# 128 unused bytes per partition behind the weight tiles of a convolution and two MLP layers on one core

## The chip, the cores and the metric

The kernel runs on one core of one Trainium2 chip. The time is the device time of one execution in microseconds. Three timed runs of the kernel before gave 2313.24, 2318.7 and 2322.2 us; their median is 2318.7 us.

## The reference

The input x is 4 sequences of 4096 tokens with 192 channels. A causal convolution of 7 taps comes first, its taps a softmax over the kernel axis with one set for each of 8 heads of 24 channels; then two MLP layers with 2048 hidden units each. Cut to what is computed:

```
w = softmax(weight, axis=-1)                              # 8 heads x 7 taps
a[b, s, h] = sum_k w[h, k] * x_padded[b, s + k, h]        # 6 zeros ahead of each sequence
h = a @ moe_w_in                                          # 16384 x 192 @ 192 x 2048
y = (h - tanh(h)) @ moe_w_out                             # 2048 x 192
out = relu(y @ moe2_w_in) ** 2 @ moe2_w_out
```

The weights of the MLPs come as float64, x and the output are float32.

## The kernel before

The tokens are cut into 32 blocks of 512. A block goes through the convolution (mostly VectorE, taps with one multiply-add each, L230 and L233; for the first blocks TensorE with diagonal weights, L254), then layer 0, then layer 1. All products keep about float32 accuracy with operands in the type float32r: each operand is split into a high part and a rest, and three products stand for one: high by high, rest by high, high by rest. `gh` and `gl` are high part and rest of the activations (L417 on ScalarE, L419 on VectorE), `z` and `y` the split inputs of layer 0 and layer 1, `wIh`, `wIl` and `wO` the split weights.

The work is laid out in units. A unit is one layer, one block and one eighth of the hidden units (256 of them): 19 matmuls in each of two row halves of the TensorE array (`pe_step`). Each half reads 64 partitions, and the two halves' matmuls alternate in the instruction stream, so that they run beside each other as pairs (`matmul`, L359). The weight load belongs to each matmul. The order is written out by hand (`tc.manual_schedule`): between the matmuls of a unit stand its activation (`act`), its splits (`split`) and small lists of side work (`side`), such as loading and convolving later blocks, decoding float64 weights (`decode_ops`, L124 to L160, in the first 200 us only) and finishing an earlier block. Where one half hands a PSUM bank to the other, a no-operation on GpSimd carries the signal (`relay`); twice GpSimd zeroes the head of `xTa` and `xTb` for a new sequence (`halo`, L258).

DMAs all go by the SP queue: x into `xa`, `xb` and once into `t`, in pieces of 128 bytes (`load_a`, `load_b`); float64 weights into `st` (`load_w`); one half of `z` and `y` copied to the other 64 partitions, 4096 bytes each (`other_half`, L289); and the output from `ua` and `tu`, in pieces of 128 bytes (`store`, L442).

Tiles are given their place in SBUF in the order of the pools, each tile's size being rounded up to 32 bytes. In the program's list of allocations the tiles begin as follows (byte within each partition, and the remainder after division by 512; weights within a tile are read in blocks of 512 bytes from its start):

| tiles | first byte | remainder | size of one |
|---|---|---|---|
| wIh0, wIl0, wO0, wIh1, wIl1, wO1 | 16512, 28800, 41088, 65664, 77952, 90240 | 128 | 12288, wO 24576 |
| wt, taps, warm, mx, sm, th, den | 114816 to 115040 | | 4 to 56 |
| st (2), da (2) | 115072, 127360 | 384 | 6144, 3072 |
| xb, xa | 133504, 135552 | 384 | 2048 |
| xTb (2) | 137600, 139680 | 384, 416 | 2072 |
| xTa (2) | 141760, 143840 | 448, 480 | 2072 |
| accA, accB, z (2), y (3), t (3), gh (6), gl (6), ua, tu | 145920 to 223744 | 0 | 2048, z and y 8192 |

Of the kernel before, what the change touches and what calls it, by code (L numbers as in the profile page):

```python
# [10 lines left out]
F32 = mybir.dt.float32  # L11
# [19 lines left out]
def conv_mlp_mlp_kernel(ctx: ExitStack, tc: tile.TileContext, x, weight, w_in1, w_out1, w_in2, w_out2, out):  # L31
# [17 lines left out]
    P = 128  # L49
# [14 lines left out]
    wpool = ctx.enter_context(tc.tile_pool(name="wpool", bufs=1))  # L64
# [13 lines left out]
    for m in range(2):  # L78
        W.append(
            dict(  # L80
                Ih=wpool.tile([P, NP, CI], F32R, name=f"wIh{m}"),
                Il=wpool.tile([P, NP, CI], F32R, name=f"wIl{m}"),
                O=wpool.tile([P, NP, 2, 2 * D], F32R, name=f"wO{m}"),
            )
        )
    w_in = [w_in1, w_in2]
    w_out = [w_out1, w_out2]
    staged = {}
# [524 lines left out]
```

## Time and profile before

| | |
|---|---|
| median of three timed runs | 2318.7 us |
| lowest and highest of them | 2313.24 and 2322.2 us |
| span of the profiled execution | 2316.5 us |
| instructions | 50386 |
| TensorE matmul busy | 2301.4 us, 99% of the span |
| ScalarE busy | 1618.3 us, 70% |
| VectorE busy | 1468.0 us, 63% |
| GpSimd busy | 1.4 us |

The span is the time from the first to the last instruction of one profiled execution; the median of the timed runs is 2.2 us above it. Busy time of TensorE counts matmuls whose ends are modelled and overlap, so that 99% says that it hardly ever waited, not that it ran at its peak. PE is TensorE's matmul, PEld its weight load, DVE VectorE, ACT ScalarE, POOL GpSimd, SPq the queue that issues DMAs.

### The profile page before, as it was taken

The page shows a single profiled execution, that of the slowest core. Times are in us where ns is not written, and L with a number is a line of the kernel's source. Part 1 is how long each engine was busy: PE and PEld are TensorE (multiplying, and loading weights), DVE is VectorE, ACT ScalarE, POOL GpSimd, SP SyncE. Part 2 cuts the span into 40 slices and gives each one's busy share as a digit, 9 for nine tenths or more (in the row PEclk, how much of TensorE's full clock was granted, in tenths as well). Part 3 has the DMA queues.
Part 4 walks back from the last instruction along what each step waited for, and adds up shares of the span by engine and source line. Part 5 has one row for each costly group of instructions (what it writes and reads, how often), then busy time and mean ns, then how long its engine had stood idle before and what let it go on. Part 6 is the DMA issues. An engine that isn't in the chain of part 4 may idle for free.

```text
span 2316.5 us, 50386 instructions
## 1 busy us (share of the span) xinstructions
PE 2301.4 (99%) x19500; PEld 2046.9 (88%) x19500; DVE 1468.0 (63%) x2299; ACT 1618.3 (70%) x2866; POOL 1.4 (0%) x15
## 2 busy tenths in 40 slices
PE   9999999999999999999999999999999999999999
PEld 6777888888888888889999999999999999999998
DVE  8988666655576665666556665566665557665553
ACT  5577766677766777766777667776667776677766
POOL 0000000000000000000000000000000000000000
PEclk8999999999999999999999999999999999999999
DMA  5221111110110100101101011011111011110000
GB/s 128 64 75 36 22 22 17 22 23 14 22 22 17 26 15 17 27 13 26 22 11 26 17 22 22 15 22 22 17 22 24 13 22 18 21 22 15 13 13 15
DMA packets 216863, 57.78 MB, mean 25 GB/s; under 512 B 204336, under 2 KB 210480, under 8 KB 216624
## 3 DMA queue, kind: packets, MB, share of 16 engines
q1 hardware_dynamic: 216624, 54.56, 11.8%
q8 instruction: 154, 2.52, 0.5%
q14 instruction: 85, 0.70, 0.1%
HBM read 25.17 MB, written 12.58 MB: 16 GB/s over the span
## 4 chain that ended last, share of the span: by engine, by line
PE 96%; DVE 2%; ACT 1%; issue 0%; SPq 0%; DMA 0%; DVEq 0%; ACTq 0%
PE ph L359 45%; PE pA L359 31%; PE pB L359 20%; DVE da L138 0%; DVE da L134 0%; ACT gh L417 0%; DVE t L406 0%; DVE accA L233 0%; SPq L218 0%; ACT da L124 0%; DMA t<-in_x 0%; ACT t L408 0%; DVE da L129 0%; DVE gl L419 0%; DVE t L410 0%
## 5 line engine op out<-in xcount | busy, mean ns | idle before, releaser
L359 PE MATMUL pA<-gh,wO 64*128 64x512 f32 x4088 | 1281.7, 393 | 0.0
L419 DVE TENSOR_TENSOR gl<-t,gh 128x512 fp32r<-128x512 f32 x1024 | 682.3, 688 | 622.0 <-ACT gh L417 597.8
L359 PE MATMUL ph<-z,wIh 64*128 64x512 f32 x3072 | 990.0, 394 | 7.6 <-DVE t L406 6.4
L359 PE MATMUL ph<-y,wIh 64*128 64x512 f32 x3072 | 981.1, 392 | 0.6 <-DVE t L410 0.6
L359 PE MATMUL pB<-gh,wO 64*128 64x512 f32 x2044 | 802.3, 392 | 0.0
L359 PE MATMUL pA<-gl,wO 64*128 64x512 f32 x2044 | 801.4, 392 | 0.0
L359 PE MATMUL pB<-gl,wO 64*128 64x512 f32 x2044 | 800.4, 392 | 0.0
L359 PEld LDWEIGHTS pA<-gh,wO 64*128 64x128 f32 x4088 | 738.7, 185 | 47.4 <-issue 0.4
L417 ACT CAST gh<-t 128x512 fp32r<-128x512 f32 x1024 | 604.5, 614 | 97.8 <-DVE t L406 94.9
L359 PE MATMUL ph<-z,wIl 64*128 64x512 f32 x1536 | 604.3, 394 | 0.0
L359 PE MATMUL ph<-y,wIl 64*128 64x512 f32 x1536 | 601.6, 392 | 0.1
L359 PEld LDWEIGHTS ph<-z,wIh 64*128 64x128 f32 x3072 | 554.2, 186 | 48.7 <-ACT wIh L150 5.0
L359 PEld LDWEIGHTS ph<-y,wIh 64*128 64x128 f32 x3072 | 549.8, 185 | 36.3 <-DVE t L410 1.2
L405 ACT ACTIVATE t<-ph 128x512 f32<-128x512 f32 x512 | 305.4, 598 | 358.4 <-PE ph L359 278.9
L406 DVE TENSOR_TENSOR t<-ph,t 128x512 f32<-128x512 f32 x512 | 351.6, 689 | 199.2 <-ACT t L405 197.9
L359 PEld LDWEIGHTS pB<-gh,wO 64*128 64x128 f32 x2044 | 378.4, 185 | 36.2
L408 ACT ACTIVATE t<-ph 128x512 f32<-128x512 f32 x512 | 305.3, 596 | 147.3 <-PE ph L359 123.4
L359 PEld LDWEIGHTS pA<-gl,wO 64*128 64x128 f32 x2044 | 378.1, 185 | 26.7 <-DVE gl L419 0.4
L359 PEld LDWEIGHTS pB<-gl,wO 64*128 64x128 f32 x2044 | 378.4, 185 | 24.7
L412 ACT ACTIVATE t<-t 128x512 f32<-128x512 f32 x504 | 318.6, 632 | 16.0
L359 PEld LDWEIGHTS ph<-z,wIl 64*128 64x128 f32 x1536 | 285.6, 186 | 17.9 <-DVE wIl L155 0.7
L359 PEld LDWEIGHTS ph<-y,wIl 64*128 64x128 f32 x1536 | 284.1, 185 | 17.6 <-DVE wIl L155 0.4
(71 smaller groups left out, 707.0 us busy)
## 6 DMA issues: line engine op xcount, KB each, us to landing
z<-z SPq DMA_DIRECT2D x32, 256.0 KB, 2.9
y<-y SPq DMA_DIRECT2D x32, 256.0 KB
out<-ua SPq DMA_DIRECT2D x128, 64.0 KB, 1.9
xa<-in_x SPq DMA_DIRECT2D x124, 64.0 KB, 2.3
st<-in_moe_w_out SPq DMA_DIRECT2D x16, 384.0 KB, 6.3
xb<-in_x SPq DMA_DIRECT2D x64, 64.0 KB, 2.3
st<-in_moe_w_in SPq DMA_DIRECT2D x16, 256.0 KB, 3.2
out<-tu SPq DMA_DIRECT2D x64, 64.0 KB, 1.9
```

The source lines that it names most:

```text
L359: ins = nc.tensor.matmul(o, w, r, start=start, stop=stop).ins
L405: nc.scalar.activation(t, ph, AF.Tanh)
L406: nc.vector.tensor_tensor(t, ph, t, op=ALU.subtract)
L408: nc.scalar.activation(t, ph, AF.Relu)
L412: nc.scalar.activation(t, t, AF.Square)
L417: nc.scalar.copy(gh, t)
L419: nc.vector.tensor_tensor(gl, t, gh.bitcast(F32), op=ALU.subtract)
```

## The change

One tile is added to the pool of the weights, behind them and ahead of the small tiles of the taps. It has 32 float32 in each partition and is neither written nor read. No instruction is added.

```
                 O=wpool.tile([P, NP, 2, 2 * D], F32R, name=f"wO{m}"),
             )
         )
+    wpool.tile([P, 32], F32, name="pad")
     w_in = [w_in1, w_in2]
     w_out = [w_out1, w_out2]
     staged = {}
```

The weights stay where they are, and every tile behind them begins 128 bytes further on: the remainders 384, 416, 448, 480 and 0 of the table become 0, 32, 64, 96 and 128. PSUM is not touched.

## Rows read from the trace of the kernel before

**Rows 1.** The page: busy time of each engine, with share of the span and count.

```profile
PE 2301.4 (99%) x19500; PEld 2046.9 (88%) x19500; DVE 1468.0 (63%) x2299; ACT 1618.3 (70%) x2866; POOL 1.4 (0%) x15
```

**Rows 2.** The page: chain that ended last, share of the span by engine.

```profile
PE 96%; DVE 2%; ACT 1%; issue 0%; SPq 0%; DMA 0%; DVEq 0%; ACTq 0%
```

**Rows 3.** Stretches: length; busy us (instructions) per engine; granted TensorE clock; DMA.

```profile
30.00:40.00 10.00, 9.27 (x27) 6.49 (x26) 9.57 (x17) 4.54 (x8) 0.00 (x0) 0.50 0.50 142
...
100.00:200.00 100.00, 97.43 (x820) 75.91 (x818) 86.02 (x143) 76.84 (x141) 0.00 (x0) 1.00 0.26 70
200.00:400.00 200.00, 200.00 (x1726) 162.43 (x1724) 133.44 (x207) 139.37 (x248) 0.00 (x0) 1.00 0.12 22
400.00:1000.00 600.00, 600.00 (x5168) 487.33 (x5166) 369.06 (x572) 427.15 (x754) 0.20 (x2) 1.00 0.11 20
1000.00:1064.00 64.00, 64.00 (x554) 51.99 (x552) 36.74 (x56) 45.81 (x81) 0.00 (x0) 1.00 0.11 20
1064.00:2000.00 936.00, 936.00 (x8028) 897.61 (x8026) 584.77 (x906) 656.04 (x1157) 0.40 (x4) 1.00 0.11 20
2000.00:2280.00 280.00, 280.00 (x2403) 268.90 (x2401) 157.65 (x243) 198.12 (x347) 0.00 (x0) 1.00 0.07 15
```

**Rows 4.** Instructions in order around 800 us, TensorE: start us, duration us, engine, line.

```profile
800.12 0.39 PE L359 MATMUL pA<-gl,wO 64*128 64x512 f32 x1
800.12 0.39 PE L359 MATMUL ph<-z,wIl 64*128 64x512 f32 x1
800.35 0.40 PE L359 MATMUL pA<-gh,wO 64*128 64x512 f32 x1
800.35 0.40 PE L359 MATMUL ph<-z,wIh 64*128 64x512 f32 x1
800.59 0.39 PE L359 MATMUL pA<-gh,wO 64*128 64x512 f32 x1
```

**Rows 5.** The same around 1200 us.

```profile
1200.57 0.39 PE L359 MATMUL ph<-y,wIl 64*128 64x512 f32 x1
1200.61 0.40 PE L359 MATMUL pA<-gh,wO 64*128 64x512 f32 x1
1200.80 0.39 PE L359 MATMUL ph<-y,wIh 64*128 64x512 f32 x1
```

**Rows 6.** Instructions in order on GpSimd, in the middle of the span.

```profile
1064.28 0.10 POOL L258 MEMSET xTa<- 128x6 f32 x1 [564.94 <-PE pA L359]
```

**Rows 7.** Weight loads of the convolution on TensorE, in order; one moving read each.

```profile
9.14 0.19 PEld L254 LDWEIGHTS ph<-xTb,y 128*128 128x128 f32 x1 [0.24 <-ACT y L248]
...
13.00 0.19 PEld L254 LDWEIGHTS ph<-xTb,y 128*128 128x128 f32 x1 [0.24 <-issue]
...
14.58 0.19 PEld L254 LDWEIGHTS ph<-xTa,y 128*128 128x128 f32 x1 [0.24 <-issue]
...
19.31 0.19 PEld L254 LDWEIGHTS ph<-xTa,y 128*128 128x128 f32 x1 [0.24 <-issue]
```

**Rows 8.** Groups by line and shape: busy us, mean ns | idle before, releaser.

```profile
L419 DVE TENSOR_TENSOR gl<-t,gh 128x512 fp32r<-128x512 f32 x1024 | 682.3, 688 | 622.0 <-ACT gh L417 597.8 <-PE ph L359 0.5
L155 DVE TENSOR_TENSOR wIl<-da,wIh 128x384 fp32r<-128x384 f32 x16 | 8.9, 556 | 1.2 <-ACT wIh L150 1.2
L160 DVE TENSOR_TENSOR wO<-da,wO 128x256 fp32r<-128x256 f32 x16 | 6.7, 419 | 0.6 <-ACT wO L150 0.6
L160 DVE TENSOR_TENSOR wO<-da,wO 128x128 fp32r<-128x128 f32 x16 | 4.6, 285 | 0.0
```

**Rows 9.** DMA issues: count, KB each, median us from issue to landing.

```profile
z<-z SPq DMA_DIRECT2D x32, 256.0 KB, 2.9
st<-in_moe_w_in SPq DMA_DIRECT2D x16, 256.0 KB, 3.2
```

**Rows 10.** Who waited in the first 200 us: us in total, times, longest.

```profile
PE ph L359 <- DVE t L406: 6.4, 6, 3.2
DVE xTa L265 <- DMA t<-in_x: 3.2, 1, 3.2
```

More of the change, by code (lines that the diff above doesn't have):

```diff
@@ L85, in conv_mlp_mlp_kernel @@
         )
+    wpool.tile([P, 32], F32, name="pad")
     w_in = [w_in1, w_in2]
```

## The prediction

> **What bounds the kernel now.** I began with the busy times of the engines [rows 1] and the chain that ended last [rows 2]. TensorE is busy 99% of the span and holds 96% of the chain, VectorE 2%, ScalarE 1%, DMA nothing that shows. That names the engine; what one pair of matmuls costs it has to be read from a stretch without waits. The stretches [rows 3] give it: from 200 to 2280 us TensorE is busy in every microsecond, at a granted clock of 1.00 (the upper level, 2.4 GHz). In that time it starts 1726 + 5168 + 554 + 8028 + 2403 = 17879 matmuls, or 8940 pairs, one in each row half: 2080 us / 8940 = 232.7 ns a pair. So 90% of the time is one number times a count, and the change can matter in two ways: it alters that number, or it alters the first 200 us, in which TensorE does wait (6.4 us for VectorE's t in all, [rows 10]) and VectorE is busy 86.02 of 100 us [rows 3].
>
> The stretches show something else that I need for the range. The pair is not equally long everywhere: 600 / (5168 / 2) = 232.2 ns from 400 to 1000 us, 936 / (8028 / 2) = 233.2 ns from 1064 to 2000 us. The instructions in order show what differs. Around 800 us both matmuls of a pair start at the same hundredth [rows 4], around 1200 us one starts 0.04 us behind the other [rows 5]. The trace changes from the one to the other at about 1064 us, where GpSimd, which also carries the signals between the halves, zeroes the heads of two tiles [rows 6]. That nothing else sets it off I can't show from one execution.
>
> **The change part by part.** One tile is declared, and nothing reads or writes it. It removes, adds and moves no instruction, no DMA, no wait, so the sum over instructions is zero times anything. What is left is the place of the operands. Weights stay, at 128 bytes past a multiple of 512; everything behind them is read and written 128 bytes further on. Each kind of user of those tiles is a term:
>
> (a) TensorE's moving reads of z, y, gh and gl, from remainder 0 to remainder 128. No matmul of the trace in the long stretch reads a moving operand from remainder 128, so I bound it. Below: the 512 columns need 512 / 2.4 = 213.3 ns at the granted clock, which is 232.7 - 213.3 = 19.4 ns less, x 8940 = -173 us. Above: the slowest regular moving reads of the trace are those of the convolution, a weight load every 0.43 us [rows 7], 430 - 232.7 = 197 ns more, x 8940 = +1764 us. The ends are far apart, and the row that tells most about addresses is the upper one itself: those reads are of unsplit float32, which accounts for no address, but they start at xT plus 0, 4, ... 24 bytes, in tiles that begin at remainders 384 (xTb) and one of 448 and 480 (xTa). From 9.14 to 13.00 us there are 9 loads in 3.86 us, from 14.58 to 19.31 us 11 in 4.73 us: 0.429 and 0.430 us each, whatever the start. I take 0.
>
> (b) VectorE and ScalarE. VectorE's subtraction shows both kinds of address: between weight tiles and da (remainders 128 and 384) it takes 285, 419 and 556 ns for 128, 256 and 384 elements, some 136 ns for each 128 more, so 692 ns for 512; between t, gh and gl (remainder 0) the 512 take 688 ns [rows 8]. That is 0.6% at most, and of no certain sign: in the first 200 us, where VectorE is on the path, 0.006 x 200 = 1.2 us either way. Behind 200 us TensorE hides it: from 400 to 1000 us VectorE works 369 of 600 us and ScalarE 427 [rows 3], so ScalarE would have to become 600 / 427 = 1.4 times as slow before it bound anything. I take 0.
>
> (c) DMAs. z and y copies land 2.9 us after their issue and the largest loads of input weights 3.2 us [rows 9]; behind 200 us they are lost in the stretch without waits. In the first 200 us one DMA is waited for visibly, 3.2 us by VectorE's first use of t [rows 10]. So the bounds are -3.2 us (that wait gone) and +2.9 us (a copy twice as long, wholly on the path); the pieces of x keep their size and order, and I take 0.
>
> On (c) the Trainium skill has a rule, DMA: Bandwidth & Descriptors, "How a descriptor splits into AXI transactions": a transfer is cut at 256-byte boundaries, and one that starts off them needs a transaction more. By it the 4096-byte copies of z and y would go from 16 to 17 transactions, and the 2048-byte pieces of the weights, which now start off a boundary, from 9 to 8. No row here separates aligned from unaligned copies of one size. The sum by the rule, as an estimate from that page, would be 2.9 / 16 = 0.2 us more a copy and 3.2 / 9 = 0.4 us less a load, both under cover but for the first few, so some 2318 us instead of 2318.7 us.
>
> Sum: 2316.5 us of span plus 0. The timed median lies 2.2 us above that span, so the forecast is **2318.7 us**, as before.
>
> What one execution of the same program can do: if the halves stayed together to the end, the 8028 + 2403 matmuls behind 1064 us (5216 pairs) would each save 1.0 ns: 2316.5 - 5.2 = 2311.3 us. If they parted at 200 us, the 3724 pairs before 1064 us would each pay it: 2320.2 us. With the 2.2 us on top that is 2313.5 to 2322.4 us, and the timed runs reach from 2313.24 to 2322.2 us. That is the likeliest case's own range: a shift of addresses has no hold on it that I see, but the median of a few runs may land anywhere in it.
>
> **The rivals.**
>
> *Slower: load and moving read meet.* After the change the weights and the moving operands begin at the same remainder, 128, while a weight load (128 columns, 512 bytes) runs beside moving reads. If SBUF serves two readers at like offsets worse, every pair pays. The place is each pair of the long stretch, and the price is taken from the widest spacing of neighbouring pairs in the rows, 0.24 us (800.35 to 800.59, [rows 4]): 240 - 232.7 = 7.3 ns x 8940 = +65 us, 2384 us. It decides from 11.6 / 8940 = 1.3 ns a pair. For it: no row has the two at one remainder. Against it: each weight block starts at 128, 640, 1152 or 1664 in every 2048 bytes while moving tiles start at 512 there, and no row shows another spacing for one of the four; and the convolution's reads above don't care.
>
> *Faster: the present place is the bad one.* The pair stands 19.4 ns above its columns. If a part of that comes from where the operands lie, moving them may give it back, up to the -173 us of (a): 2145 us. Against it: the moving tiles lie in fourteen and more places of remainder 0, beside weights in four places of every 2048 bytes, and the trace keeps one spacing; nothing ties the 19.4 ns to an address. The Trainium skill speaks for it in a way: TensorE: Matmul & The Clock Gate, "Back-to-back issue gap", gives N/2.4 + 2.5 ns, so 215.8 ns here, and the rows show 232.7 ns. By that rule as the whole cost the time would be about 2318.7 - 8940 x 0.0169 = 2168 us, an estimate; the trace disagrees with it today, for a cause that it doesn't name.
>
> *The start shifts.* The first 200 us hold waits of several engines on each other, and TensorE's granted clock falls to 0.50 from 30 to 40 us [rows 3], in which 27 matmuls start where 86 start at full rate. A change of (b) or (c) by a microsecond could lengthen that idle time and cost one more such stretch: (86 - 27) / 2 x 0.2327 = +6.9 us, 2325.6 us, or save as much, 2311.8 us. Both are inside 0.5%.
>
> *The change does nothing of what it says:* an unused tile gets no room, or the rounding swallows it. Then the time is that of before, 2318.7 us, and no run of times tells it from the forecast; only the addresses would.
>
> **How the numbers follow.** A measurement of this kernel can tell about 0.5%, 11.6 us, from no change. The forecast has 0.79, with the idle tile inside it; the shifted start 0.05, on either side of it and within 0.5%; load and moving read 0.10; the present place 0.06. So faster 0.06, same 0.84, slower 0.10. The range must hold the likeliest case's 2313.5 to 2322.4 us and the shifted start on both sides, 2311.8 to 2325.6 us; together 0.84, so it need not reach the two outer rivals. I round it to 2311 to 2327 us, the upper side a little wider because the slower rival can also be small.
>
> **What would show it.** Right: 19500 matmuls as before, 232 to 233.5 ns a pair between 200 and 2280 us, VectorE's 512-element subtraction at 688 ns within a few, copies of z at about 2.9 us. The time at which one half falls behind the other may be another; then the time is off by 1.0 ns for each pair in between. Wrong: a pair spacing that is off by more than 1.3 ns in both kinds of stretch alike (an address matters to TensorE), or one operation of VectorE or ScalarE with another duration at the same shape while TensorE begins to wait behind 200 us.

## The result, and the profile after

The changed kernel takes 2261.22 us (2261.17 to 2261.57, four runs) beside 2315.97 us for the kernel before (2313.01 to 2322.2, four runs): a ratio of 0.9762, with a 95% interval from 0.9742 to 0.9782. It is faster by 2.4%, where no change was forecast. The profiled execution has a span of 2259.4 us, 57.1 us less.

The page of the changed kernel, busy time per engine and the chain that ended last; the number of instructions is the same as in [rows 1]:

```profile
PE 2242.7 (99%) x19500; PEld 1917.7 (85%) x19500; DVE 1464.7 (65%) x2299; ACT 1616.1 (72%) x2866; POOL 1.4 (0%) x15
...
PE 93%; DVE 4%; ACT 2%; issue 1%; SPq 0%; DMA 0%; DVEq 0%; ACTq 0%
```

TensorE is still the bound, and VectorE and ScalarE do the same work in nearly the same time. Busy time alone can't show what changed: its share is 99% in both. The stretches do. Each line has the stretch, its length, then busy time and number of instructions per engine (TensorE's matmul, its weight load, VectorE, ScalarE, GpSimd), granted clock and DMA:

```profile
0.00:200.00 200.00, 188.73 (x1412) 149.93 (x1414) 174.37 (x300) 130.47 (x248) 0.82 (x9) 0.96 0.32 83
...
200.00:400.00 200.00, 200.00 (x1768) 165.31 (x1766) 135.80 (x211) 143.89 (x257) 0.00 (x0) 1.00 0.12 22
400.00:1000.00 600.00, 600.00 (x5298) 495.88 (x5296) 381.14 (x592) 433.31 (x765) 0.20 (x2) 1.00 0.11 21
1000.00:1064.00 64.00, 64.00 (x568) 54.13 (x566) 39.04 (x63) 46.95 (x83) 0.20 (x2) 1.00 0.12 22
1064.00:2000.00 936.00, 936.00 (x8262) 828.62 (x8261) 594.00 (x922) 677.36 (x1195) 0.20 (x2) 1.00 0.11 20
2000.00:2220.00 220.00, 220.00 (x1944) 194.78 (x1942) 127.31 (x197) 158.69 (x279) 0.00 (x0) 1.00 0.07 14
```

The granted clock is 1.00 in both kernels from 200 us on, so it is not the clock. In 600 us TensorE now has 5298 matmuls where it had 5168 [rows 3]: 226.5 ns a pair for 232.2. From 200 to 2220 us there are 17840 matmuls, 8920 pairs, in 2020 us: 226.5 ns, for 232.7 before. The 8940 pairs of the stretch of before thus save 6.2 ns each, 55 of the 57.1 us of span. (A matmul that crosses an edge is counted on both sides of it. Taken in one piece, 200 to 2220 us hold 17826 matmuls now and 17350 before, 226.6 and 232.9 ns: the difference is the same.) The first 200 us hold as many matmuls as before but for 4, at the same mean clock of 0.96; the line of the kernel before:

```profile
0.00:200.00 200.00, 190.22 (x1408) 150.57 (x1410) 174.04 (x299) 129.97 (x247) 0.82 (x9) 0.96 0.32 83
```

Instructions in order on TensorE, around 800 and around 1200 us of the changed kernel (start us, duration us):

```profile
800.20 0.39 PE L360 MATMUL ph<-y,wIh 64*128 64x512 f32 x1
800.20 0.39 PE L360 MATMUL pA<-gl,wO 64*128 64x512 f32 x1
800.43 0.39 PE L360 MATMUL ph<-y,wIh 64*128 64x512 f32 x1
800.43 0.39 PE L360 MATMUL pA<-gh,wO 64*128 64x512 f32 x1
800.65 0.39 PE L360 MATMUL ph<-y,wIl 64*128 64x512 f32 x1
...
1200.49 0.39 PE L360 MATMUL ph<-z,wIl 64*128 64x512 f32 x1
1200.51 0.39 PE L360 MATMUL pA<-gh,wO 64*128 64x512 f32 x1
1200.72 0.39 PE L360 MATMUL ph<-z,wIh 64*128 64x512 f32 x1
```

In these lines pairs follow each other every 0.22 or 0.23 us, and none takes the 0.24 us that stood in [rows 4]. The halves part here too (0.02 us at 1200 us), but the spacing is the same in both stretches: 600 / 2649 = 226.5 ns and 936 / 4131 = 226.6 ns. The weight loads show what runs beside what. Around 800 us of the changed kernel:

```profile
800.20 0.18 PEld L360 LDWEIGHTS ph<-y,wIh 64*128 64x128 f32 x1
800.21 0.18 PEld L360 LDWEIGHTS pA<-gh,wO 64*128 64x128 f32 x1
800.43 0.18 PEld L360 LDWEIGHTS ph<-y,wIl 64*128 64x128 f32 x1
800.43 0.18 PEld L360 LDWEIGHTS pA<-gh,wO 64*128 64x128 f32 x1
```

The next matmul's load starts with the matmul of its own half, so that for 0.18 us TensorE reads weights and a moving operand through the same 64 partitions.

### The profile page after: what moved, and what is told of

It reads as the page before. It is cut to its first block, busy times and chain, and to the rows that moved or that the text cites. A ratio compares the mean times of both kernels' runs of the same rounds, so it can differ in the third digit from the quotient of the medians.

```text
span 2259.4 us, 50386 instructions
## 1 busy us (share of the span) xinstructions
PE 2242.7 (99%) x19500; PEld 1917.7 (85%) x19500; DVE 1464.7 (65%) x2299; ACT 1616.1 (72%) x2866; POOL 1.4 (0%) x15
## 4 chain that ended last, share of the span: by engine, by line
PE 93%; DVE 4%; ACT 2%; issue 1%; SPq 0%; DMA 0%; DVEq 0%; ACTq 0%
PE ph L360 44%; PE pA L360 29%; PE pB L360 20%; DVE t L407 1%; ACT gh L418 1%; DVE da L139 1%; DVE da L135 1%; DVE gl L420 0%; DVE accA L234 0%; ACT t L409 0%; ACT da L125 0%; DVE wIl L156 0%; SPq L219 0%; DVE da L130 0%; ACT t L413 0%
## 5 line engine op out<-in xcount | busy, mean ns | idle before, releaser
L360 PE MATMUL pA<-gh,wO 64*128 64x512 f32 x4088 | 1255.6, 387 | 0.2 <-ACT gh L418 0.2
L360 PEld LDWEIGHTS pA<-gh,wO 64*128 64x128 f32 x4088 | 752.2, 184 | 65.7 <-ACT gh L418 1.0
L360 PE MATMUL pB<-gh,wO 64*128 64x512 f32 x2044 | 790.1, 387 | 0.0
L360 PE MATMUL pA<-gl,wO 64*128 64x512 f32 x2044 | 789.9, 386 | 0.0
L360 PE MATMUL pB<-gl,wO 64*128 64x512 f32 x2044 | 789.5, 386 | 0.0
L360 PEld LDWEIGHTS ph<-z,wIh 64*128 64x128 f32 x3072 | 567.6, 185 | 64.0 <-DVE t L407 6.2
L360 PEld LDWEIGHTS ph<-y,wIh 64*128 64x128 f32 x3072 | 565.3, 184 | 51.3 <-DVE t L411 1.7
L360 PE MATMUL ph<-z,wIl 64*128 64x512 f32 x1536 | 596.1, 388 | 0.0
L360 PE MATMUL ph<-y,wIl 64*128 64x512 f32 x1536 | 593.2, 386 | 0.1
```

The lines of the kernel that those rows point to most:

```text
L360: ins = nc.tensor.matmul(o, w, r, start=start, stop=stop).ins
```

## The experiments

Theory A, formed on this result: what counts is where a moving operand lies *relative to the weights*. Rivals: its own remainder counts (B), or that of the other engines' tiles, which moved too (C). All kernels are the kernel before with other pads; each was run once with a profile. The kernel before, on the same chips, took 2313.0 to 2313.3 us beside eight of them and 2321.4 us beside seven. So the times alone can't tell a few us apart, and the reading rests on the spacing: that of the stretch from 400 to 1000 us, 600 us over half the number of matmuls in the line; its columns are those above.

**Pad ahead of the weights** (p_ahead128):

```
+    wpool.tile([P, 32], F32, name="pad0")
     W = []
```

Expected: 

> The 128 unused bytes stand ahead of the weights, so weights and all other tiles move together: weights to remainder 256 of 512, moving operands to 128. Theory A (what counts is where the moving operand lies relative to the weights): the relation is that of the kernel before, so 232 to 233.2 ns a pair and 2313 to 2322 us. Theory B (what counts is the moving operand's own remainder): 226.7 ns a pair and 2261 us, as with the pad behind the weights. Theory C (it is the tiles of VectorE, ScalarE and the DMAs, whose remainders also move): 2261 us, as B.

```profile
400.00:1000.00 600.00, 600.00 (x5168) 485.90 (x5166) 369.06 (x573) 427.27 (x754) 0.20 (x2) 1.00 0.11 20
1000.00:2000.00 1000.00, 1000.00 (x8610) 825.23 (x8608) 624.22 (x967) 704.01 (x1240) 0.40 (x4) 1.00 0.11 20
```

Measured 2313.0 us, 232.2 ns. Every tile but the weights lies where the changed kernel has it, and the gain is gone: B and C fall for this pad.

**384 bytes ahead, 128 behind** (p_a384_b128):

```
+    wpool.tile([P, 96], F32, name="pad0")
     W = []
...
+    wpool.tile([P, 32], F32, name="pad")
     w_in = [w_in1, w_in2]
```

Expected: 

> 384 unused bytes ahead of the weights and 128 behind them: weights at remainder 0 of 512, all other tiles 512 bytes further on than in the kernel before, so at their old remainders. Theory A (relative place of moving operand and weights): the relation is that of the changed kernel, both at one remainder, so 226.7 ns a pair and 2261 us. Theory B (moving operand's own remainder) and theory C (tiles of the other engines): 232 to 233.2 ns, 2313 to 2322 us.

```profile
400.00:1000.00 600.00, 600.00 (x5298) 495.88 (x5296) 381.06 (x593) 432.89 (x765) 0.20 (x2) 1.00 0.11 21
```

Measured 2261.05 us, 226.5 ns, with every tile but the weights at its old remainder of 512. With the run above this settles A for these two relations, 0 and 128 bytes.

**Other pads behind the weights.** Only the number in the added line changes, for example for 256 bytes (p_b256):

```
+    wpool.tile([P, 64], F32, name="pad")
     w_in = [w_in1, w_in2]
```

512 bytes: 

> 512 unused bytes behind the weights instead of 128. If the place counts only by its remainder after division by 512 (the weights are read in blocks of 512 bytes), theory A and B both expect the time of the kernel before, 2313 to 2322 us and 232 to 233.2 ns a pair. If any shift against the weights helps, or the remainder of a larger power of two counts, 2261 us or another value.

256 bytes: 

> 256 unused bytes behind the weights: moving operands at remainder 256, weights at 128. Theory A with a period of 512: a third relation, (moving minus weights) = 128 instead of 384 (before) or 0 (changed kernel), so a time of its own is possible, 2250 to 2330 us; with a period of 256 it is the relation of before, 2313 to 2322 us. Theory B with a period of 256: moving operands at a multiple of 256 as before, 2313 to 2322 us.

64 bytes: 

> 64 unused bytes behind the weights: moving operands at remainder 64, 64 bytes short of the weights' 128. If only the equal remainder is good: 2313 us, 232 ns a pair. If the cost falls off with the distance (384 before, 64 here, 0 with the pad of 128): between 2261 and 2313 us.

160 bytes: 

> 160 unused bytes behind the weights: moving operands at remainder 160, 32 bytes past the weights' 128. If only the equal remainder is good: 2313 us, 232 ns a pair. If the good place is a window that begins at the weights' remainder (the moving read ahead of the load that runs beside it): 2261 us, or less.

384 bytes: 

> 384 unused bytes behind the weights: moving operands at remainder 384, 256 bytes from the weights' 128. If the good relation repeats every 256 bytes: 226.7 ns a pair, 2261 us. If only the equal remainder of 512 is good: 232.4 ns (as at distances of 128 either way) or 233.3 ns (as at 64 and 32), 2313 to 2322 us. Anything under 226.7 ns would show a better place than the changed kernel's.

192 bytes: 

> 192 unused bytes behind the weights: moving operands 64 bytes past the weights. If the cost depends on the distance alone and not on its sign: as 64 bytes short of them, 233.3 ns a pair and 2322 us. If a moving read ahead of its load is better than one behind it: under 2313 us.

32 bytes: 

> 32 unused bytes behind the weights: moving operands at remainder 32, which is 160 past the weights in a period of 256. If every distance other than 0 (mod 256) costs like 128, 192 and 32 did: 232.4 to 233.3 ns a pair, 2313 to 2322 us. If 64 past the weights (2281 us) is one of a row of cheaper places: between 2261 and 2290 us.

96 bytes: 

> 96 unused bytes behind the weights: 224 past the weights (32 short of them) in a period of 256. If nearness counts: near 2261 us. If 32 short is as bad as 32 past: 233.3 ns a pair, 2322 us. Under 226.7 ns a pair it would beat the changed kernel.

224 bytes: 

> 224 unused bytes behind the weights: 96 past the weights in a period of 256, between 64 (228.9 ns a pair) and 128 (232.4 ns). If the cost rises between them: 229 to 232.4 ns a pair, 2281 to 2313 us. Otherwise, as at 32 past: 233.3 ns, 2322 us. Under 226.7 ns a pair it would beat the changed kernel.

The same stretch of 384 bytes:

```profile
400.00:1000.00 600.00, 600.00 (x5296) 495.87 (x5294) 381.20 (x592) 433.24 (x765) 0.20 (x2) 1.00 0.11 21
```

of 192 bytes:

```profile
400.00:1000.00 600.00, 600.00 (x5248) 491.92 (x5245) 378.07 (x587) 430.52 (x761) 0.20 (x2) 1.00 0.12 21
```

of 256 bytes:

```profile
400.00:1000.00 600.00, 600.00 (x5168) 485.89 (x5166) 369.00 (x572) 427.40 (x754) 0.20 (x2) 1.00 0.11 20
```

of 32 bytes:

```profile
400.00:1000.00 600.00, 600.00 (x5126) 481.96 (x5124) 366.20 (x567) 424.75 (x748) 0.20 (x2) 1.00 0.11 20
```

and of 64, 96 and 160 bytes:

```profile
400.00:1000.00 600.00, 600.00 (x5146) 480.32 (x5144) 367.12 (x569) 425.99 (x752) 0.20 (x2) 1.00 0.11 20
400.00:1000.00 600.00, 600.00 (x5146) 483.02 (x5144) 367.04 (x570) 426.26 (x753) 0.20 (x2) 1.00 0.11 20
400.00:1000.00 600.00, 600.00 (x5148) 482.19 (x5146) 367.36 (x569) 426.18 (x752) 0.20 (x2) 1.00 0.11 20
```

The whole row, ordered by how far the moving operands begin past the weights, in a period of 256 bytes (the times are of one run each, but for the change and the kernel before):

| distance | pad | us | matmuls in 600 us | ns a pair |
|---|---|---|---|---|
| 0 | 128 (the change) | 2261.22 | 5298 | 226.5 |
| 0 | 384 | 2261.3 | 5296 | 226.6 |
| 32 | 160 | 2321.9 | 5148 | 233.1 |
| 64 | 192 | 2281.41 | 5248 | 228.7 |
| 96 | 224 | 2321.66 | 5146 | 233.2 |
| 128 | 0 (before) | 2315.97 | 5168 | 232.2 |
| 128 | 256 | 2313.21 | 5168 | 232.2 |
| 128 | 512 | 2313.01 | 5166 | 232.3 |
| 160 | 32 | 2330.95 | 5126 | 234.1 |
| 192 | 64 | 2321.73 | 5146 | 233.2 |
| 224 | 96 | 2321.54 | 5146 | 233.2 |

Pads of 128 and 384 agree, as do those of 0, 256 and 512: at distances 0 and 128 the relation repeats every 256 bytes, which was only one of the cases held open for 384. Three pads came out as no case expected: those of 64 and 160 are dearer than the kernel before, and that of 32 is the dearest of all (by their spacing, 233.1 to 234.1 ns). Neither nearness nor the sign explains the row: 32 past and 32 short are both dear, 64 past is cheap and 64 short is not. No multiple of 32 beats distance 0, so no kernel here clearly beats the changed one.

What the row leaves open: the weights stay at remainder 128 in all of it, and weights and operands were moved together, or the weights alone, only at distances 0 and 128. That the distance decides is shown for these two. For the other six it could also be the operand's own remainder.

**Only gh and gl, or only z and y** (p_w128, p_z128_w384). For the first:

```
+    work.tile([P, 32], F32, name="padw", bufs=1)
     w_in = [w_in1, w_in2]
```

and for the second:

```
+    zp.tile([P, 32], F32, name="padz", bufs=1)
+    work.tile([P, 96], F32, name="padw", bufs=1)
     w_in = [w_in1, w_in2]
```

Expected of the first: 

> 128 unused bytes ahead of t, gh and gl only: gh and gl lie at the weights' remainder (128), z and y at 0 as before. In 18 of the 19 pairs of a unit one half reads gh or gl while the other reads z or y. Sum theory (each moving read that lies off its weights costs by itself, 10220 of the 19436 are mended): 2313 - 0.526 x 52 = 2286 us, about 229 ns a pair. Pair theory (the pair is as long as its slower half, 1 pair in 19 is mended): 2313 - 52/19 = 2310 us, 232 ns a pair.

Expected of the second: 

> The mirror case: z and y at remainder 128 with the weights, t, gh and gl moved by 512 bytes and so at 0 as before. Sum theory: 9216 of 19436 moving reads are mended, 2313 - 0.474 x 52 = 2288 us. Pair theory: 2313 us, 232 ns a pair (no pair has both halves reading z or y).

The stretch of the first:

```profile
400.00:1000.00 600.00, 600.00 (x5201) 516.07 (x5199) 372.20 (x578) 429.57 (x758) 0.20 (x2) 1.00 0.11 20
```

and of the second:

```profile
400.00:1000.00 600.00, 600.00 (x5208) 517.08 (x5206) 373.80 (x580) 429.41 (x759) 0.20 (x2) 1.00 0.11 20
```

Measured 2300.14 and 2296.47 us, 230.7 and 230.4 ns. Both theories of the pair missed: against 2313.02 us the two gain 12.9 and 16.6 us, together 29.5, where both kinds mended gain 52 us. So mending one read of a pair gives back 13 or 17 us, and mending the other as well a further 35 to 39. The second kernel moves z and y alone to another remainder, so it also shows that the moving operands themselves are enough.

**Which half counts** (p_split, p_cross). Both put wO elsewhere than wIh and wIl:

```
+                _=wpool.tile([P, 96], F32, name=f"pado{m}"),
                 O=wpool.tile([P, NP, 2, 2 * D], F32R, name=f"wO{m}"),
             )
         )
+        wpool.tile([P, 32], F32, name=f"padi{m}")
```

p_split then has 128 bytes behind the weights and 384 ahead of t, gh and gl; p_cross only 128 ahead of t, gh and gl.

Expected of p_split: 

> wIh and wIl stay at remainder 128 and z and y go to 128; wO goes to 0 and gh and gl stay at 0. So within a row half each moving read has its own kind of weights at its remainder (34 of 38 matmuls of a unit; 4 are followed by a load of the other kind), while against the other half's weights it lies 128 bytes off. Theory 'own half' (a load disturbs the moving read of the same half, through the same partitions): close to 226.7 ns, 2261 to 2268 us. Theory 'any half' (a load disturbs the moving reads of both): about 232 ns, 2308 to 2313 us.

Expected of p_cross: 

> The weights as in the kernel that keeps each kind with its own operands (wIh, wIl at 128, wO at 0), but z and y at 0 and gh and gl at 128: each moving read lies 128 bytes off the weights of its own half and equal with those of the other half. Theory 'own half': 232.4 ns a pair, 2308 to 2313 us (the 4 of 38 matmuls at the changes are mended). Theory 'any half, the other counts': 2261 to 2268 us.

The stretch of p_split:

```profile
400.00:1000.00 600.00, 600.00 (x5272) 554.79 (x5270) 379.23 (x590) 431.97 (x763) 0.20 (x2) 1.00 0.11 21
```

and of p_cross:

```profile
400.00:1000.00 600.00, 600.00 (x5161) 490.84 (x5160) 368.95 (x572) 426.67 (x753) 0.20 (x2) 1.00 0.11 20
```

Measured 2271.05 us (227.6 ns) and 2315.14 us (232.5 ns). The relation works within a row half: equal to one's own weights gives back nearly all, equal to the other half's nothing. The two also rule out that the moving reads of the two halves disturb each other by their own distance: they lie 128 bytes apart in both kernels, in the fast one and in the slow one.

p_split lies 3 us above what 'own half' expected, p_cross 2 us. The trace of p_split shows where its excess sits. Starts of one half's matmuls around 804 us:

```profile
803.25 0.39 PE L363 MATMUL ph<-y,wIh 64*128 64x512 f32 x1
...
804.61 0.39 PE L363 MATMUL ph<-y,wIh 64*128 64x512 f32 x1
804.85 0.39 PE L363 MATMUL pA<-gh,wO 64*128 64x512 f32 x1
805.08 0.39 PE L363 MATMUL pA<-gh,wO 64*128 64x512 f32 x1
805.30 0.39 PE L363 MATMUL pA<-gl,wO 64*128 64x512 f32 x1
```

The six spacings up to 804.61 us take 1.36 us, 227 ns each; the three across the change from y to gh take 0.69 us, 230 ns each. Worked out from all starts between 400 and 1000 us, 14 of the 19 places of a unit stand at 226.7 ns, as all 19 do in the changed kernel, and only the five at or right behind a change of kind take 228.8 to 232.5 ns. Every matmul of p_split lies equal with the weights that it uses itself; what differs at a change is the load that runs beside it. That points to this load, of the next matmul's weights, as the one that the relation is about.

## Why the prediction was wrong

The bound was read rightly: one pair spacing times 8940 pairs. The step that failed is the choice of 0 in term (a), "TensorE's moving reads ... from remainder 0 to remainder 128". The bounds given for it hold (-173 to +1764 us), and the measured term is -55 us. What misled me is the row that the choice rested on. The convolution's reads [rows 7] start at seven addresses in each tile and keep 0.43 us, but they repeat only every 430 ns, where a stall of the size found here may lie under other cover (no run tests that); and they were not the case to be judged, a weight load and a moving read of one half that run beside each other at 233 ns a pair. A row of another operation with another spacing says little about a contention.

The other argument, that the trace of before keeps one spacing over many places, was empty: all weights lay at 128 and all moving operands at 0 of 512, so every matmul in the long stretch had the same distance, 128 of 256. The table of addresses ahead of the prediction showed that; I read it for one operand at a time, and the relation is between two.

Terms (b) and (c) were right as far as the rows show. VectorE's subtraction takes 688 ns as in [rows 8], and copies and loads land as in [rows 9]; groups and DMA issues of the changed kernel:

```profile
L420 DVE TENSOR_TENSOR gl<-t,gh 128x512 fp32r<-128x512 f32 x1024 | 682.3, 688 | 593.6 <-ACT gh L418 569.7
```

```profile
z<-z SPq DMA_DIRECT2D x32, 256.0 KB, 2.9
st<-in_moe_w_in SPq DMA_DIRECT2D x16, 256.0 KB, 3.2
```

So no run here shows the further transaction that the Trainium skill (DMA: Bandwidth & Descriptors, "How a descriptor splits into AXI transactions") gives to a transfer that starts off a 256-byte boundary: z copies moved off it land in 2.9 us as before, and the estimate of 0.2 us more would have stood out. The prediction's "from 9 to 8" for the loads of the weights takes the rule for the side that is written, of which that page of the Trainium skill says nothing; these loads land in 3.2 us as before too. Another dependence on the address does show: copies of z land in 3.0 us in the six kernels whose z lies off every multiple of 128 bytes (pads of 32, 64, 96, 160, 192 and 224), and in 2.9 us in all others. The line of the pad of 64 bytes:

```profile
z<-z SPq DMA_DIRECT2D x32, 256.0 KB, 3.0
```

Of the rivals, the faster one was the case, with a chance of 0.06 and the price left at its far bound: it returned 6.2 of the 19.4 ns above the columns. What the other 13 ns are stays open. The 215.8 ns that the prediction took for this rival from the Trainium skill (TensorE: Matmul & The Clock Gate, "Back-to-back issue gap") are given there for a matmul by itself; no long stretch here comes under 226.5 ns. The slower rival had the right pair of operands and the wrong sign: it took the equal remainder for the bad place, and it is the good one. A rival stated as "the distance between them counts", with no sign, would have covered both. The shifted start did not come.

The account of the spread between executions held in its numbers. In p_ahead128 the spacing stays at 232.2 to 232.3 ns (1000 / 4305) to 2000 us, and it takes 2313.0 us; 2313.5 us was worked out for halves that stay together, and they all but do:

```profile
1200.07 0.39 PE L360 MATMUL ph<-y,wIl 64*128 64x512 f32 x1
1200.08 0.39 PE L360 MATMUL pA<-gh,wO 64*128 64x512 f32 x1
```

In the changed kernel the halves part after GpSimd's zeroing, at 1043 us:

```profile
1042.70 0.10 POOL L259 MEMSET xTa<- 128x6 f32 x1 [551.04 <-PE pA L360]
1043.11 0.10 POOL L259 MEMSET xTb<- 64x6 f32 x1 [0.31 <-POOL xTa L259]
```

There the lag is only 0.02 us. In p_a384_b128, where the distance is 0 too, it is as long as in the kernel before, and the spacing is 1000 / 4413 = 226.6 ns for 226.5 ahead of it:

```profile
1000.00:2000.00 1000.00, 1000.00 (x8826) 992.44 (x8824) 632.78 (x982) 723.88 (x1277) 0.40 (x4) 1.00 0.11 20
```

```profile
1200.36 0.39 PE L361 MATMUL ph<-z,wIl 64*128 64x512 f32 x1
1200.41 0.39 PE L361 MATMUL pA<-gh,wO 64*128 64x512 f32 x1
```

The changed kernel's four runs lie within 0.4 us, those of before within 9.2 us. So a lag of some 0.04 us costs 1.0 ns a pair at distance 128 and hardly anything at distance 0; at the other distances no lag as long was seen.

What starts the lag is open. The prediction tied it to the zeroing at 1064 us. But the text ahead of it counts too few zeroings: the trace of the kernel before has three behind the start, at 499, 1064 and 1632 us, and behind that of 499 us the halves are still together [rows 4].

```profile
499.14 0.10 POOL L258 MEMSET xTa<- 128x6 f32 x1 [497.73 <-PE pA L359]
```

In p_ahead128 they stay within 0.01 us of each other behind the one at 1064 us, as shown above.

## What to carry to other kernels

Where TensorE is the bound and each matmul has its own weight load, it is worth listing the byte addresses of both operands and taking their difference modulo 256; in this kernel, the only one tested, an equal place gave 226.5 ns a pair and other multiples of 32 gave 228.7 to 234.1, so a tile added or dropped anywhere in between can move the whole kernel by 1 to 3%. When a change adds no instruction, compare the spacing of pairs and not the busy share, and judge an address by the relation of the two operands that are read at the same time. And before one version is called faster for its edit, see whether the edit also moved the tiles.

## What the runs showed of the hardware

A weight load and a moving read of the same row half, running side by side, are not independent: with float32r operands, 64 rows and 512 columns, the spacing of a pair ran from 226.5 to 234.1 ns with nothing but the places of tiles changed. Between the distances 0 and 128, which repeat after 256 bytes, the distance alone decides: 226.5 or 232.2 ns. Which part of the chip makes it so is not shown. The last matmuls, which use all 128 rows and have gh, gl and wO at one remainder, are still some 0.23 us apart in the changed kernel, as they are in the kernel before (0.69 us from the first to the fourth of four there, as here):

```profile
2250.42 0.39 PE L360 MATMUL pA<-gl,wO 128*128 128x512 f32 x1
2250.65 0.40 PE L360 MATMUL pB<-gh,wO 128*128 128x512 f32 x1
2250.89 0.39 PE L360 MATMUL pB<-gl,wO 128*128 128x512 f32 x1
2251.11 0.40 PE L360 MATMUL pB<-gh,wO 128*128 128x512 f32 x1
```

The kernel before, first and fourth of four:

```profile
2307.74 0.40 PE L359 MATMUL pB<-gh,wO 128*128 128x512 f32 x1
...
2308.43 0.39 PE L359 MATMUL pB<-gl,wO 128*128 128x512 f32 x1
```

Three spacings in 0.69 us are 230 ns in both kernels, at distance 0 and at 128, so the rule found for the halves was not shown to hold for full rows; the program has only 20 matmuls of this form.
